# A sign bit carried through a float64-to-float32 conversion: a parametric ReLU on ScalarE in place of an absolute value, and one VectorE operation less

## The chip, the cores and the metric

The kernel runs on one core of one Trainium2 chip. Time is device microseconds (us) of one execution. Before the change the median of three runs is 1049.24 us (1047.91 to 1050.06). In the text PE is TensorE, ACT is ScalarE, DVE is VectorE, POOL is GpSimd, and SP is the engine whose queue issues all DMAs here.

## The reference, cut to what matters

Three stages follow each other: block-causal attention (4 batches, 8 heads, 576 positions, head size 64), a feed-forward layer with h - tanh(h), and a gated layer with an RMS norm in front.

```
scores = where(mask, scale * q @ k^T, -1e9); attn = softmax(scores); x = attn @ v     # q, k, v are float32
h = x @ w_in;  x = (h - tanh(h)) @ w_out                                              # (2304,512)@(512,2048)@(2048,512)
xn = x / sqrt(mean(x*x) + 1e-6) * rms_g
out = (silu(xn @ w_gate) * (xn @ w_val)) @ w_out2                                     # 512 -> 1536 -> 512
```

The weights w_in, w_out, w_gate, w_val and the last w_out arrive as float64. The chip's engines work on float32, so the kernel itself turns each weight into float32 (and then into a rounded high part and a remainder, since nearly every product is computed as three matmuls: high times high, high times low, low times high).

## The kernel before, in words

**The conversion.** A float64 number is read as two 32-bit words. `convert` takes a staged block of 128 x 1024 words, that is 128 x 512 numbers, and runs four operations, each over 128 x 512 elements: ACT multiplies the high word, read as a float, by 2^-112 and takes the absolute value (line 140); ACT scales the low word down to its top three bits (line 142); DVE clamps the first result to a range (line 143), shifts it left by three bits and ors the low bits in (line 144), and then takes the sign bit from the staged high word and ors it in (line 145). The tile `st` is the staging buffer that the DMA of line 129 fills, `cv` holds the intermediate value, `cu` the low bits, and the result lands in `w` (a weight of the first layer), in `fu` (a weight group of the gated layer) or stays in `cv` where the split into high and low part follows in `convert` itself.

**Who calls it.** First-layer weights: 16 blocks of w_in and 16 of w_out, by `convert1`, through the first part of the attention (7 blocks are spread over the first attention unit) and the first pass of the first layer. Gated layer: the 6 pairs of w_out2 blocks during the middle passes, and 12 pairs of w_gate/w_val blocks (one pair is a weight group) around the change from the first layer to the gated one. The class `Convert` loads a pair, converts it, splits it, forms sums of its quarters on POOL (lines 752 to 756), and splits these.

**The stretch that matters late.** The gated layer walks twelve weight groups j. Group 0 to 2 and 10, 11 are used in a form with seven half-size products (`fast`), groups 3 to 9 of the first pass in the plain form with eight (`plain`, 48 matmuls of 384 columns). The weights stand in three slots (`ws`). Groups 3 to 9 are converted while the products run: in step j the kernel fills the slot of group j+2 from the converted pair, writes back what it has split (`keep`, line 774, and `send`, line 782, both DMAs out of `ws` and `wc` to DRAM), converts the second block of group j+3, and loads and converts the first block of group j+4. Groups 10 and 11 are read back from DRAM into their slots (line 1045).

**Order.** PE runs in the order written. ACT, DVE, POOL and SP are placed by a scheduler that simulates a timeline when the program is built; what `pin` wraps keeps its order among pinned instructions. From group 10 of the first pass on, DVE, ACT and POOL run in written order too. All DMAs go through SP, one after the other: a DMA whose data isn't ready holds up those behind it.

Of the kernel before, what the change touches and what calls it, by code (L numbers as in the profile page):

```python
# [10 lines left out]
F32 = mybir.dt.float32  # L11
F32R = mybir.dt.float32r
BF16 = mybir.dt.bfloat16
I32 = mybir.dt.int32
U32 = mybir.dt.uint32
ALU = mybir.AluOpType
AF = mybir.ActivationFunctionType
# [11 lines left out]

REBIAS = 2.0 ** -112  # L30
LOWBITS = 2.0 ** -29 * (1 - 2.0 ** -20)
SIGN = -0x80000000
HIGHEST = float(np.array([0x47EFFFFF], np.uint32).view(np.float32)[0])


# [58 lines left out]
def build(ctx, tc, q, k, v, w_in, w_out, w_gate, w_val, w_out2, rms_g, ident_in, out):  # L94
    nc = tc.nc
    pin = tc.keep_in_program_order
    PE, ACT, DVE, POOL, SP = nc.tensor, nc.scalar, nc.vector, nc.gpsimd, nc.sync
    w_in, w_out, w_gate, w_val, w_out2 = (a.bitcast(I32) for a in (w_in, w_out, w_gate, w_val, w_out2))

    def rnd(eng, o, i):  # L100
        if eng is ACT:
            ACT.activation(out=o, in_=i, func=AF.Copy)  # L102
        else:
            eng.tensor_copy(out=o, in_=i)

    def lo(eng, o, full, hi):
        eng.tensor_tensor(out=o, in0=full, in1=hi.bitcast(F32), op=ALU.subtract)  # L107
# [24 lines left out]
    def convert(st, h, l=None):  # L132

        e = st.rearrange("p (e t) -> p e t", t=2)
        low, high = e[:, :, 0], e[:, :, 1]
        t = wk.tile([128, 512], I32, name="cv", tag="cv")
        u = wk.tile([128, 512], I32, name="cu", tag="x2s")
        f = t.bitcast(F32)

        pin(ACT.activation(out=f, in_=high.bitcast(F32), func=AF.Abs, scale=REBIAS))  # L140

        pin(ACT.activation(out=u, in_=low.bitcast(U32), func=AF.Copy, scale=LOWBITS, bias=-0.5))
        pin(DVE.tensor_scalar(f, f, HIGHEST * REBIAS, 0.0, ALU.min, ALU.max))
        DVE.scalar_tensor_tensor(t, t, 3, u, ALU.logical_shift_left, ALU.bitwise_or)
        DVE.scalar_tensor_tensor(h.bitcast(I32) if l is None else t, high, SIGN, t, ALU.bitwise_and, ALU.bitwise_or)
        if l is None:
            return
        rnd(ACT, h, f)
        lo(DVE, l, f, h)
# [445 lines left out]
    with tc.manual_schedule(engines={PE.engine}):  # L595
# [37 lines left out]
        def convert1(n):  # L633

            j, half = divmod(n, 2)
            if half == 0:
                t = w1tile(0, j)
                convert(staged.pop(n), t[:, 0:512], t[:, 512:1024])
                SP.dma_start(out=w1d[0][j], in_=t.bitcast(F32))
                wi[j] = t  # L640
                return
            if j % 2 == 0:
                wo["new"] = w1tile(1, j + 1, F32)
            t = wo["new"]
            o = t[:, 512 * (j % 2):512 * (j % 2) + 512]
            convert(staged.pop(n), o)
            wo[j] = o
            if j % 2:
                SP.dma_start(out=w1f[j // 2], in_=t)
# [84 lines left out]
        class Convert:  # L734
# [8 lines left out]
            def piece(self, part):  # L743
                if part == 0:
                    self.f = env["cvp"].tile([128, 2, 512], F32, name="fu", tag="fu", bufs=2)
                convert(self.st[part], self.f[:, part])
# [145 lines left out]
        for s in range(NSA):  # L892
# [32 lines left out]
            h = env["t"].tile([128, 512], F32, name="t", tag="t")[:, 0:TG]  # L925
# [385 lines left out]
```

## Time and profile before

| | |
|---|---|
| median of three runs | 1049.24 us |
| profiled execution, its own time | 1049.75 us |
| its span in the profile | 1048.0 us |
| PE busy | 1025.0 us, 98% |
| DVE busy | 782.4 us, 75% |
| ACT busy | 665.3 us, 63% |
| POOL busy | 351.4 us, 34% |

The span is the time from the first to the last instruction that the profile shows; the execution's own time has 1.75 us more around it. Busy shares are means over stages that differ, so the table of stretches and the waits of each engine matter more than the totals. A row of waits says which instruction waited, for which one, for how long in total, how often, and the longest.

### The profile page before, as it was taken

What the parts mean: (1) busy time and instruction counts of PE and PEld (TensorE: products, weight loads), DVE (VectorE), ACT (ScalarE), POOL (GpSimd) and SP (SyncE); (2) the same over time, 40 slices, a digit from 0 to 9 for tenths busy, and PEclk for the clock granted to TensorE, in tenths of its full rate; (3) what the DMA queues carried; (4) which work ended last, traced back from release to release, by engine and by line L of the source; (5) the groups of instructions that cost most, each with busy time, mean ns of one, the idle gap of its engine ahead of it and who ended that gap; (6) DMA issues with size and microseconds to landing.
All of it is one profiled execution on the core that took longest, in us unless ns stands there. A gap on an engine that the chain in (4) does not pass through costs nothing.

```text
span 1048.0 us, 18044 instructions
## 1 busy us (share of the span) xinstructions
PE 1025.0 (98%) x6014; PEld 934.5 (89%) x6014; DVE 782.4 (75%) x1557; ACT 665.3 (63%) x1533; POOL 351.4 (34%) x467
## 2 busy tenths in 40 slices
PE   8899999999999999999999999999999999999998
PEld 5666678998889889998999989998999999999998
DVE  5988857776787786778667989877876678666775
ACT  6977768788888877788858675543742147422253
POOL 5622111123343233424332544347211281111710
PEclk9999999999999999999999999999999999999999
DMA  9898898989787699768859978799697757876664
GB/s 215 272 293 296 263 301 261 277 224 287 203 231 193 152 268 279 210 204 260 295 162 340 372 281 330 262 350 347 241 345 270 273 196 262 299 278 247 257 218 145
DMA packets 190958, 274.03 MB, mean 261 GB/s; under 512 B 109456, under 2 KB 151184, under 8 KB 184464
## 3 DMA queue, kind: packets, MB, share of 16 engines
q1 hardware_dynamic: 190864, 272.87, 79.4%
q8 instruction: 48, 0.79, 0.3%
q14 instruction: 46, 0.38, 0.1%
HBM read 209.39 MB, written 63.44 MB: 260 GB/s over the span
## 4 chain that ended last, share of the span: by engine, by line
PE 74%; DVE 9%; DMA 8%; ACT 5%; issue 3%; POOL 1%; SPq 1%; DVEq 0%; POOLq 0%; ACTq 0%
PE t L930 5%; PE t L482 5%; PE t L932 5%; PE t L931 5%; PE acc L706 4%; PE acc L708 4%; PE acc L707 4%; PE gv L1026 4%; PE gv L1028 4%; PE gv L1027 4%; PE t L526 3%; PE acc L716 3%; PE ga L708 2%; PE ga L706 2%; PE ga L707 2%
## 5 line engine op out<-in xcount | busy, mean ns | idle before, releaser
L930 PE MATMUL t<-xh,w 128*128 128x384 f32 x384 | 137.3, 357 | 1.5 <-DVE pp L107 1.4
L932 PE MATMUL t<-xh,w 128*128 128x384 f32 x384 | 129.6, 338 | 0.0
L931 PE MATMUL t<-xl,w 128*128 128x384 f32 x384 | 129.3, 337 | 0.0
L1026 PE MATMUL gv<-xh,ws 128*128 128x384 f32 x308 | 103.5, 336 | 2.7 <-DMA ws<-w2d 2.4
L1028 PE MATMUL gv<-xh,ws 128*128 128x384 f32 x308 | 103.4, 336 | 0.0
L1027 PE MATMUL gv<-xl,ws 128*128 128x384 f32 x308 | 103.4, 336 | 0.0
L706 PE MATMUL acc<-w,gh 128*128 128x512 f32 x240 | 98.6, 411 | 1.2 <-ACT gh L102 0.9
L497 ACT ACTIVATE pt<-pt,stat 128x64 f32<-128x64 f32 (+2 forms) x144 | 80.3, 559 | 25.9 <-DVE pt L495 24.9
L708 PE MATMUL acc<-w,gl 128*128 128x512 f32 x240 | 95.0, 396 | 0.6 <-DVE gl L107 0.6
L707 PE MATMUL acc<-w,gh 128*128 128x512 f32 x240 | 94.4, 393 | 0.0
L1080 ACT ACTIVATE gt<-c 128x384 f32<-128x384 f32 x29 | 15.2, 524 | 116.7 <-DVE c L1079 116.7
L1083 POOL TENSOR_TENSOR g<-va,vb 128x384 f32<-128x384 f32 x29 | 31.8, 1095 | 150.0 <-ACT va L1082 150.0
L495 DVE TENSOR_SCALAR_CACHE_REDUCE pt<-t 128x64 f32<-128x64 f32 (+2 forms) x144 | 64.0, 449 | 19.7 <-PE t L482 18.8
L930 PEld LDWEIGHTS t<-xh,w 128*128 128x128 f32 x384 | 72.3, 188 | 5.8 <-DVE pp L107 1.8
L931 PEld LDWEIGHTS t<-xl,w 128*128 128x128 f32 x384 | 72.4, 189 | 2.3
L932 PEld LDWEIGHTS t<-xh,w 128*128 128x128 f32 x384 | 72.0, 188 | 0.0
L102 ACT ACTIVATE pp<-t 128x512 fp32r<-128x512 f32 (+6 forms) x152 | 63.0, 436 | 11.7 <-PE t L526 11.3
L526 PE MATMUL t<-ident,pt 128*128 128x128 f32 x400 | 65.7, 274 | 2.2 <-POOL pt L511 2.2
L107 DVE TENSOR_TENSOR gl<-gt,gh 128x384 fp32r<-128x384 f32 x80 | 55.4, 693 | 15.5 <-ACT gh L102 15.1
L107 DVE TENSOR_TENSOR pp<-t,pp 128x512 fp32r<-128x512 f32 (+3 forms) x112 | 55.0, 509 | 14.9 <-ACT pp L102 14.4
L107 POOL TENSOR_TENSOR vp<-vr,vp 128x640 fp32r<-128x640 f32 (+1 forms) x24 | 33.7, 1406 | 95.0 <-ACT vp L102 89.1
L526 PEld LDWEIGHTS t<-ident,pt 128*128 128x128 f32 x400 | 50.5, 140 | 16.4 <-issue 5.1
(210 smaller groups left out, 3183.1 us busy)
## 6 DMA issues: line engine op xcount, KB each, us to landing
ws<-w2d SPq DMA_DIRECT2D x26, 1792.0 KB, 7.3
w<-w1d_i SPq DMA_DIRECT2D x68, 512.0 KB, 5.5
ws<-wod SPq DMA_DIRECT2D x21, 1536.0 KB, 6.4
w<-w1d_o SPq DMA_DIRECT2D x52, 512.0 KB, 5.1
st<-in_moe_w_out SPq DMA_DIRECT2D x28, 512.0 KB, 4.5
w2d<-wc SPq DMA_DIRECT2D x9, 1024.0 KB, 6.6
st<-in_moe_w_in SPq DMA_DIRECT2D x16, 512.0 KB, 5.1
w1d_i<-w SPq DMA_DIRECT2D x16, 512.0 KB, 5.0
```

What stands on the lines that cost most here:

```text
L107: eng.tensor_tensor(out=o, in0=full, in1=hi.bitcast(F32), op=ALU.subtract)
L497: ACT.activation(out=pt[:, 0:keys], in_=pt[:, 0:keys], func=AF.Exp, scale=-1.0, bias=least, accum_out=st[:, 8 + ti:9 + ti])
L526: PE.transpose(t[:, (j - a) * 128:(j - a + 1) * 128], pt[:, j * 128:(j + 1) * 128], ident)
L706: PE.matmul(acc, lhsT=gh[:, c], rhs=wh, start=first, stop=False, skip_group_check=more)
L707: PE.matmul(acc, lhsT=gh[:, c], rhs=wl, start=False, stop=False, skip_group_check=more)
L708: PE.matmul(acc, lhsT=gl[:, c], rhs=wh, start=False, stop=last, skip_group_check=more)
L930: PE.matmul(h, lhsT=wh[:, c], rhs=xh[:, kk], start=(kk == 0), stop=False)
L931: PE.matmul(h, lhsT=wh[:, c], rhs=xl[:, kk], start=False, stop=False)
L932: PE.matmul(h, lhsT=wl[:, c], rhs=xh[:, kk], start=False, stop=(kk == KD - 1))
L1026: PE.matmul(ps, lhsT=wh[:, c], rhs=xh[:, kk], start=(first and kk == 0), stop=False)
L1027: PE.matmul(ps, lhsT=wh[:, c], rhs=xl[:, kk], start=False, stop=False)
L1028: PE.matmul(ps, lhsT=wl[:, c], rhs=xh[:, kk], start=False, stop=(last and kk == nk - 1))
```

## The change: what it does

The absolute value becomes a parametric ReLU with slope 2^32 for negative inputs. A positive high word gives the same value as before. A negative one gives a value that is 2^32 times as large in size, so bit 28 of the result is set, besides its own sign bit. The shift by three moves bit 28 to bit 31, the place of the sign, and drops the old sign bit. The clamp gets a negative lower bound for that reason. The operation of line 145 goes, and line 144 writes its result where line 145 wrote it.

```diff
-SIGN = -0x80000000
+NEGATIVE = 2.0 ** 32
...
-        pin(ACT.activation(out=f, in_=high.bitcast(F32), func=AF.Abs, scale=REBIAS))
+        pin(ACT.activation(out=f, in_=high.bitcast(F32), func=AF.Prelu, scale=REBIAS, alpha=NEGATIVE))
 
         pin(ACT.activation(out=u, in_=low.bitcast(U32), func=AF.Copy, scale=LOWBITS, bias=-0.5))
-        pin(DVE.tensor_scalar(f, f, HIGHEST * REBIAS, 0.0, ALU.min, ALU.max))
-        DVE.scalar_tensor_tensor(t, t, 3, u, ALU.logical_shift_left, ALU.bitwise_or)
-        DVE.scalar_tensor_tensor(h.bitcast(I32) if l is None else t, high, SIGN, t, ALU.bitwise_and, ALU.bitwise_or)
+        pin(DVE.tensor_scalar(f, f, HIGHEST * REBIAS, -HIGHEST * REBIAS * NEGATIVE, ALU.min, ALU.max))
+        DVE.scalar_tensor_tensor(h.bitcast(I32) if l is None else t, t, 3, u, ALU.logical_shift_left, ALU.bitwise_or)
```

Since the sign no longer comes from `st`, the staging buffer's last readers are now the two ACT operations. The scheduler places the rest anew: PE keeps its order entirely, ACT has the same instructions in another order (the five loads of activation tables among them), and POOL and SP are reordered as well. Line numbers behind line 144 are one lower in the changed kernel.

On DVE, the last weight group that is converted beside the products (group 9), before; `fu` is the converted pair, `ws` a slot, and `g_7` the result of group 7:

```order
L143 TENSOR_SCALAR cv<-cv 128x512
L144 SCALAR_TENSOR_TENSOR cv<-cv,cu 128x512
L143 TENSOR_SCALAR cv<-cv 128x512
L145 SCALAR_TENSOR_TENSOR fu<-st,cv 128x512
L1102 TENSOR_TENSOR g_7_8480<-ga,gt 128x384
L144 SCALAR_TENSOR_TENSOR cv<-cv,cu 128x512
L145 SCALAR_TENSOR_TENSOR fu<-st,cv 128x512
L107 TENSOR_TENSOR ws<-fu,ws 128x1024
L1102 TENSOR_TENSOR g_7_8510<-gv,gt 128x384
L107 TENSOR_TENSOR wc<-fu,wc 128x1024
```

The same place now:

```order
L143 TENSOR_SCALAR cv<-cv 128x512
L1101 TENSOR_TENSOR g_6_8340<-gv,gt 128x384
L144 SCALAR_TENSOR_TENSOR fu<-cv,cu 128x512
L143 TENSOR_SCALAR cv<-cv 128x512
L1101 TENSOR_TENSOR g_6_8370<-gv,gt 128x384
L144 SCALAR_TENSOR_TENSOR fu<-cv,cu 128x512
L107 TENSOR_TENSOR ws<-fu,ws 128x1024
L107 TENSOR_TENSOR wc<-fu,wc 128x1024
L1101 TENSOR_TENSOR g_7_8412<-ga,gt 128x384
```

Two operations are gone, and the conversion of group 9 now stands beside the results of group 6 where it stood beside those of group 7.

On SP's queue, the end of the same stretch, before; `w2d_80` and `w2d_81` are the copies in DRAM of groups 8 and 9, `w2d_82` and `w2d_83` those of groups 10 and 11, and `xn` is the next block of activations:

```order
L774 DMA w2d_80<-ws 256x1x768
L1045 DMA ws<-w2d_82 128x3584
L774 DMA w2d_81<-ws 256x1x768
L782 DMA w2d_80<-wc 256x1x1024
L782 DMA w2d_81<-wc 256x1x1024
L1045 DMA ws<-w2d_83 128x3584
L828 DMA xn<-x2d 128x512
L829 DMA xn<-x2d 128x2x256
```

The same place now:

```order
L773 DMA w2d_80<-ws 256x1x768
L781 DMA w2d_80<-wc 256x1x1024
L1044 DMA ws<-w2d_82 128x3584
L773 DMA w2d_81<-ws 256x1x768
L827 DMA xn<-x2d 128x512
L781 DMA w2d_81<-wc 256x1x1024
L828 DMA xn<-x2d 128x2x256
L1044 DMA ws<-w2d_83 128x3584
```

The write of group 8's second part moved ahead of the load of group 10, and two loads of `xn` moved ahead of the load of group 11.

## Rows read from the trace of the kernel before

**Rows 1.** The page, busy time of each engine over the span.

```profile
PE 1025.0 (98%) x6014; PEld 934.5 (89%) x6014; DVE 782.4 (75%) x1557; ACT 665.3 (63%) x1533; POOL 351.4 (34%) x467
```

**Rows 2.** Stretches: window, length, busy us of PE, PEld, DVE, ACT, POOL, clock, DMA.

```profile
17.00:48.00 31.00, 25.72 (x164) 18.61 (x164) 27.73 (x94) 29.20 (x96) 21.73 (x45) 1.00 1.03 272
650.00:700.00 50.00, 49.46 (x283) 49.14 (x282) 41.18 (x52) 26.09 (x41) 21.92 (x22) 1.00 0.79 283
700.00:720.00 20.00, 17.58 (x100) 17.29 (x101) 12.41 (x17) 5.59 (x11) 17.26 (x17) 1.00 1.00 379
```

**Rows 3.** PE's waits, 17 to 50 us: waiter, releaser, us in total, times, longest.

```profile
PE t L579 <- ACT pp L102: 3.5, 4, 1.3
PE t L526 <- POOL pt L511: 2.2, 3, 1.3
```

**Rows 4.** PE's waits, 600 to 730 us.

```profile
PE gv L1026 <- DMA ws<-w2d: 2.4, 1, 2.4
PE acc L706 <- ACT gh L102: 0.9, 1, 0.9
PE acc L708 <- DVE gl L107: 0.6, 2, 0.3
PE ga L1028 <- DVE ws L107: 0.5, 1, 0.5
```

**Rows 5.** PE's waits, 350 to 600 us.

```profile
PE t L930 <- DVE pp L107: 1.4, 1, 1.4
```

**Rows 6.** Line 145: ns min/median/max, first and last start, shape.

```profile
L145 DVE SCALAR_TENSOR_TENSOR fu<-st,cv x36: 644/685/1819, 275.0 to 696.8; 128x512 int32<-128x512 int32 x36
L145 DVE SCALAR_TENSOR_TENSOR cv<-st,cv x16: 662/682/961, 21.3 to 134.5; 128x512 int32<-128x512 int32 x16
L145 DVE SCALAR_TENSOR_TENSOR w<-st,cv x16: 674/685/1098, 26.9 to 141.0; 128x512 int32<-128x512 int32 x16
```

**Rows 7.** DVE by line, 17 to 50 us: count, busy us, mean ns, idle before.

```profile
L145 DVE SCALAR_TENSOR_TENSOR cv<-st,cv 128x512 int32<-128x512 int32 x3 | 2.2, 727 | 0.0
L145 DVE SCALAR_TENSOR_TENSOR w<-st,cv 128x512 int32<-128x512 int32 x3 | 2.0, 683 | 0.0
```

**Rows 8.** Lines 140 and 836 on ACT: ns min/median/max.

```profile
L140 ACT ACTIVATE cv<-st x68: 642/669/743, 16.9 to 694.0; 128x512 f32<-128x512 f32 x68
...
L836 ACT ACTIVATE xn<-xn,rinv x18: 704/711/738, 563.7 to 892.1; 128x512 f32<-128x512 f32 x18
```

**Rows 9.** DVE in order of time, at 384 us: start, us, what.

```profile
384.25 0.68 DVE L145 SCALAR_TENSOR_TENSOR fu<-st,cv 128x512 int32<-128x512 int32 x1
...
385.55 0.65 DVE L107 TENSOR_TENSOR pp<-t,pp 128x512 fp32r<-128x512 f32 x1
```

**Rows 10.** DVE in order of time, groups 8 and 9.

```profile
686.90 0.69 DVE L145 SCALAR_TENSOR_TENSOR fu<-st,cv 128x512 int32<-128x512 int32 x1
...
696.78 0.69 DVE L145 SCALAR_TENSOR_TENSOR fu<-st,cv 128x512 int32<-128x512 int32 x1
...
705.09 1.23 DVE L107 TENSOR_TENSOR wc<-fu,wc 128x1024 fp32r<-128x1024 f32 x1 [2.90 <-ACT wc L761]
```

**Rows 11.** SP's queue in order of time.

```profile
687.65 0.37 SPq L129 DMA_DIRECT2D st<-in_moe_w_val  x1
...
706.96 0.70 SPq L1045 DMA_DIRECT2D ws<-w2d  x1
```

**Rows 12.** ACT in order of time, group 9's second block.

```profile
693.95 0.67 ACT L140 ACTIVATE cv<-st 128x512 f32<-128x512 f32 x1 [1.74 <-DMA st<-in_moe_w_val]
694.52 0.66 ACT L142 ACTIVATE cu<-st 128x512 int32<-128x512 uint32 x1
```

**Rows 13.** PE in order of time, first matmul of group 11.

```profile
717.97 0.42 PE L1026 MATMUL gv<-xh,ws 128*128 128x384 f32 x1 [2.42 <-DMA ws<-w2d]
```

**Rows 14.** SP's waits, 600 to 720 us.

```profile
SPq L129 <- DVE fu L145: 36.6, 12, 5.3
SPq L828 <- DMA w2d<-wc: 4.8, 2, 3.3
```

## The prediction

> **What bounds the kernel now.** I read the busy totals first. PE is busy 1025.0 of 1048.0 us; DVE, where the change takes work away, is busy 75% [rows 1]. So nearly all of what DVE saves is hidden under PE, and the change is worth what it takes from the 23 us in which PE stands still. The second view is therefore the list of PE's waits, by stretch, with the conversions in mind: these run from 17 to 141 us (first-layer weights) and in pieces from 275 to 697 us [rows 6].
>
> In the first attention unit PE loses 3.5 us to ACT and 2.2 to POOL [rows 3]. The table of stretches says who is late there: ACT is busy 29.20 of 31.00 us, DVE 27.73 [rows 2]. Between 350 and 600 us there is one wait of 1.4 us for DVE [rows 5]. Between 600 and 730 us, where the gated layer's weights are converted beside the products, PE waits 2.4 us for a DMA that loads a slot, 0.9 and 0.6 for ACT and DVE at the end of the first layer, and 0.5 for a split by DVE [rows 4]. In between PE is full, and DVE work there is free.
>
> Third, for these places, I read the engines in order of time, backwards from PE's wait to what was late. The longest one (2.4 us) ends when group 11's weights land, at 717.97 us [rows 13]. Their load left SP at 706.96 [rows 11], 11.0 us before, although the slot's last user, group 8, was through some 8 us earlier (worked out below). SP had not come to it: ahead of it in the queue stands the write of group 9's second part, whose data DVE finished only at 705.09 + 1.23 = 706.3 [rows 10]. So this wait is the tail of the conversion of group 9.
>
> **The change part by part.**
>
> *The removed operation.* 36 + 16 + 16 = 68 times a DVE operation of 0.685 us (median) goes [rows 6], 46.6 us of DVE. Directly on PE's path it stands only where a wait above ends behind it.
>
> *First unit, 17 to 48 us.* Six of them run here, 2.2 + 2.0 = 4.2 us [rows 7]. ACT's work is not reduced, and it fills all but 31.00 - 29.20 = 1.8 us [rows 2]. That is the upper bound of the gain. The lower bound is a loss of about 1: ACT's order is new here, and in it ACT takes the rounding of a converted weight a little sooner, where it can stand waiting for DVE. I take 1.0, nearer to the upper bound, since DVE at 27.73 of 31.00 us is so full that most of what ACT waits for will run through it.
>
> *First pass to 150 us, and 250 to 600 us.* The wait of 1.4 us at 384 us ends behind a run of DVE work: line 145 at 384.25, one more operation, then the awaited split at 385.55 [rows 9]. The 0.68 us of line 145 come out of that path; with the overlap of neighbours I take 0.6, between 0 (the new order puts something else there) and 1.4 [rows 5]. Everywhere else in these stretches PE's order is the same and ACT's and DVE's is partly new, so a wait of the size of the others in the lists, 1 to 2 us, can come or go; I count 0, and ±2 for the range.
>
> *End of the first layer, 600 to 650 us.* 0.9 + 0.6 us of waits for splits of the first layer [rows 4], with conversions among them on DVE. I take 0.7 of these 1.5, between 0 and 1.5. A loss of 1 is possible: behind the square root of the norm ACT now has two conversions, where it had one, before the next product's evacuation, and each can wait for its DMA (1.74 us in the row shown) [rows 12].
>
> *Groups 3 to 9.* Here the removed operation did one thing more: it was the last reader of the staging buffer. The load of the next block was issued at 687.65, right behind line 145 at 686.90 + 0.69 = 687.59 [rows 10, 11]; SP waited for that operation 12 times, 36.6 us in all [rows 14]. The loop of one group is: load issued 687.65, ACT starts on it at 693.95 [rows 12], DVE's line 145 at 696.78 [rows 10], next load. From 686.90 to 696.78 that is 9.88 us per group. PE needs 48 matmuls per group, 48 x 50 / 283 = 8.5 us [rows 2]. So the conversion falls back 1.4 us per group against PE, until PE waits for it (the 0.5 us) and the write behind it holds up SP (the 2.4 us). Without line 145 the buffer is free when ACT is through, at 694.52 + 0.66 = 695.2: the loop would be 695.2 - 687.65 = 7.5 us, shorter than PE's 8.5. PE then sets the pace, and the conversion stays ahead.
>
> How far ahead? Over the last four groups alone 4 x 1.4 = 5.6 us, so group 9's second part would be written at about 701 where it was 706.4, and the load of group 11 would leave by 701.5. Group 8's products end at about 699: 717.97 less the wait of 2.42 is 715.5, and two groups before it (9 with 48, 10 with 42 matmuls) take 90 x 0.177 = 15.9 us, with 0.5 of waiting. So the slot is free by then. With the same 11.0 us to land it is there at 712.5, and PE wants it at 715.0. What speaks against the whole 2.4: the DMA engines are full from 700 to 720 us (share 1.00) [rows 2], and the new SP order puts two loads of activations ahead of the load of group 11. I take 2.0 of the 2.4 (bounds 0 and 2.4), and 0.5 of the 0.5.
>
> *The new function on ACT.* The trace has no Prelu. Nearest rows of the same shape: the absolute value it replaces, 669 ns, and a scaling with the factor read from a tile, 711 ns [rows 8]. So a Prelu costs between 0 and 42 ns more; I take 0, since its slope is given as a number, as the scale is. The upper end, 7 x 42 ns = 0.3 us in the ACT-bound first unit, goes into the range. The Trainium skill (ScalarE: Activation LUTs, section What ACT_TABLE_LOAD costs) says that a function costs the same per element whatever it is, and that each operand read through a pointer adds about 93 ns. The two rows agree in direction and show less than half of that, 42 ns. By the page, an alpha that went in as a pointer would add 7 x 93 ns = 0.65 us in the first unit, an estimate from that page, and the sum below would be 1045.2 instead.
>
> *Sum.* 1.0 + 0.6 + 0.7 + 0.5 + 2.0 = 4.8 us. The profiled execution took 1049.75 us, its span and 1.75 us around it; less 4.8 that is 1044.95. The median of the runs is 0.5 below the profiled one, so I put the forecast between, at 1044.7.
>
> **The rivals.**
>
> *Hidden anyway.* PE is 98% busy, ACT bounds the start whatever DVE does, and the DMA engines at share 1.00 deliver group 11 no sooner, because what is issued earlier only joins a full queue. Then remain 0.6 + 0.5 and part of the first unit, 1.5 us in all: 1048.0. For it speaks the DMA row of 700 to 720 us; against it, that the share is 0.79 from 650 to 700 us [rows 2], so there is room to move the bytes forward.
>
> *All of it, and more.* If every term comes out at its upper end, and the new order takes 1.5 of the ±2 as well, the sum is 1.8 + 1.4 + 1.5 + 0.5 + 2.4 + 1.5 = 9.1 us: 1040.6. Several independent places would all have to come out well.
>
> *Slower: SP's queue.* The load of group 11 now stands behind a load of `xn`, which reuses a buffer that the write of group 8's second part must have left. SP waited for such writes before, 4.8 us over 2 times, 3.3 the longest [rows 14], but behind the load of group 11. If that wait now comes ahead of it and the conversion has not become earlier, the load leaves 3.3 us later than 706.96, and PE's wait grows from 2.4 to 5.7; the later slots, whose loads queue behind it on full DMA engines, can add as much again. With nothing gained elsewhere that is 1053 to 1056. It decides from the point at which the load of group 11 leaves SP later than 707 us.
>
> *The change doesn't do what it says*: if Prelu belonged to another set of ACT's tables, every conversion between exponentials would reload tables. The order has five such loads before and after, so I give it no chance of its own.
>
> **How the numbers follow.** Forecast (the conversion stays ahead, 1041.5 to 1047.1) 0.55; hidden anyway (1047 to 1050) 0.25; more (below 1041.5) 0.09; slower by the queue (above 1051) 0.11. What a measurement of this kernel can tell from no change is about 0.2%, 2.1 us: faster means below 1047.1, slower above 1051.3. Faster: 0.53 of the forecast, the 0.09, and 0.05 from the edge of the hidden case, 0.67. Same: the remaining 0.22. Slower: 0.11. For eight in ten the range goes from 1040.5 to 1050: it leaves out the slower case and some of the best one.
>
> **What would show it.** Right: PE's wait for the slot of group 11 is under 0.5 us, the load of that slot leaves before 703 us, and SP's wait for the conversion before a staging load is down from 36.6 us to well under 20, now on ACT. In the first unit ACT is busy over 95% of a stretch about 1 us shorter. DVE's busy total is down by 45 to 50 us, ACT's within 3 us of 665. Wrong: a Prelu over 720 ns; waits of PE at new places between 250 and 600 us that add to over 3 us; or the same 2.4 us for the slot though its load left earlier, which would make the DMA engines the cause.

## The result, and the profile after

The changed kernel takes 1040.28 us (median of 4 runs, 1039.26 to 1042.98); the kernel before, beside it, 1049.04 (1047.91 to 1050.06). The ratio is 0.9909, 95% interval 0.9891 to 0.9928: 8.8 us faster, where 4.5 were forecast. The direction was right and the size half of what came; the time lies just below the range.

The page of the changed kernel, busy time of each engine:

```profile
PE 1023.0 (98%) x6014; PEld 934.2 (90%) x6014; DVE 736.3 (71%) x1489; ACT 666.3 (64%) x1533; POOL 342.9 (33%) x467
```

Against [rows 1], DVE has 68 instructions and 46.1 us less, ACT 1.0 us more, PE the same 6014. The new function is no dearer than the old one. Its line on ACT (count, then ns min/median/max) against [rows 8]:

```profile
L140 ACT ACTIVATE cv<-st x68: 643/663/697, 14.7 to 675.3; 128x512 f32<-128x512 f32 x68
```

PE's waits from 600 to 730 us, which [rows 4] listed with 2.4 us for a DMA at their head:

```profile
PE ga L705 <- DVE va L1080: 1.0, 1, 1.0
PE acc L707 <- DVE gl L107: 0.3, 1, 0.3
PE acc L705 <- ACT gh L102: 0.2, 1, 0.2
```

The DMA wait is gone, and so are most of the waits at the end of the first layer; a wait of 1.0 us for the gate's arithmetic is new. From 350 to 600 us, where [rows 5] had one wait, the list is empty now.

SP's queue shows why the slot is in time (start, duration, what); the first row is the load of the last staged block, the second the load of group 11:

```profile
668.45 0.37 SPq L129 DMA_DIRECT2D st<-in_moe_w_val  x1
...
693.81 0.33 SPq L1044 DMA_DIRECT2D ws<-w2d  x1
```

In [rows 11] these left at 687.65 and 706.96. SP's waits from 600 to 720 us, against the 36.6 us of [rows 14]:

```profile
SPq L129 <- ACT cu L142: 16.9, 9, 3.9
...
SPq L1044 <- PE gv L1027: 8.4, 2, 5.4
...
SPq L827 <- DMA w2d<-wc: 5.8, 1, 5.8
```

The staging load now waits for ACT, and half as long. The write that the slower rival feared is waited for 5.8 us, but this wait ends at 686 us, where it holds up nobody. The load of group 11 now waits for PE's last matmul on its slot (the row of line 1044): PE sets the pace.

The stretches of [rows 2] in the changed kernel (window, length, busy us of PE, PEld, DVE, ACT, POOL, granted clock, DMA share, GB/s):

```profile
17.00:48.00 31.00, 26.21 (x148) 18.05 (x147) 23.93 (x83) 26.34 (x87) 17.27 (x40) 0.89 1.03 280
650.00:700.00 50.00, 50.00 (x287) 50.00 (x286) 30.64 (x37) 21.86 (x35) 30.29 (x29) 1.00 0.91 332
700.00:720.00 20.00, 18.99 (x114) 18.75 (x113) 13.77 (x19) 5.02 (x11) 8.95 (x8) 1.00 0.72 276
```

From 650 to 700 us PE is full, and DVE's 41.18 us are down to 30.64: the conversion is ahead. The DMA engines carry more from 650 to 700 us and are no longer full behind it. The first row is the one that went the other way: PE waits there at least as much as before, and for part of it the clock was at the lower level (1.2 GHz). PE's waits from 17 to 50 us, against [rows 3]:

```profile
PE t L578 <- ACT pp L102: 4.1, 4, 1.7
PE t L525 <- DVE xl L107: 1.3, 1, 1.3
...
PE t L525 <- POOL pt L510: 0.3, 1, 0.3
```

The waits for POOL went from 2.2 to 0.3 us, but 1.3 of this only changed its name: the last transpose of the unit waits as long as before, now with a split on DVE (`xl`) as the last thing that ends. Before, then now:

```profile
48.53 0.30 PE L526 MATMUL t<-ident,pt 128*128 128x128 f32 x1 [1.27 <-POOL pt L511]
```

```profile
49.83 0.30 PE L525 MATMUL t<-ident,pt 128*128 128x128 f32 x1 [1.27 <-DVE xl L107]
```

The waits for ACT grew from 3.5 to 4.1. Most of that is the first one. ACT takes the rounding of a converted weight (`w`) earlier now, ahead of the second rounding of `pp`, for which PE waits; before, it came behind. Before, then now:

```profile
20.49 0.85 ACT L102 ACTIVATE pp<-t 128x384 f32<-128x384 f32 x2
...
22.38 0.62 ACT L102 ACTIVATE w<-cv 128x512 fp32r<-128x512 f32 x1
```

```profile
18.67 0.62 ACT L102 ACTIVATE w<-cv 128x512 fp32r<-128x512 f32 x1
19.19 0.48 ACT L102 ACTIVATE pp<-t 128x384 f32<-128x384 f32 x1
```

PE's wait there grew from 0.95 to 1.47 us, and behind it the granted clock fell in this profile: it is 0.83 from 17 to 27 us. From 27 to 37 us, with the next long wait, it is 0.83 again. Ten us at 0.83 are 1.7 us lost, so 3.4 us went in this profile.

### The profile page after: what moved, and what is told of

It is laid out like the page before. It is cut to its first block, busy times and chain, and to the rows that moved or that the text cites. A ratio compares the mean times of both kernels' runs of the same rounds, so it can differ in the third digit from the quotient of the medians.

```text
span 1041.1 us, 17914 instructions
## 1 busy us (share of the span) xinstructions
PE 1023.0 (98%) x6014; PEld 934.2 (90%) x6014; DVE 736.3 (71%) x1489; ACT 666.3 (64%) x1533; POOL 342.9 (33%) x467
## 4 chain that ended last, share of the span: by engine, by line
PE 86%; DVE 5%; ACT 4%; DMA 2%; issue 1%; POOL 1%; SPq 1%; DVEq 0%; ACTq 0%; POOLq 0%
PE t L929 6%; PE t L931 6%; PE t L930 5%; PE t L481 5%; PE gv L1026 5%; PE gv L1027 5%; PE gv L1025 5%; PE acc L705 4%; PE acc L707 4%; PE acc L706 4%; PE acc L715 4%; PE t L525 4%; PE ga L1025 3%; PE ga L1027 3%; PE ga L1026 3%; PE ga L707 2%
## 5 line engine op out<-in xcount | busy, mean ns | idle before, releaser
L496 ACT ACTIVATE pt<-pt,stat 128x64 f32<-128x64 f32 (+2 forms) x144 | 80.5, 560 | 26.8 <-DVE pt L494 26.3
L494 DVE TENSOR_SCALAR_CACHE_REDUCE pt<-t 128x64 f32<-128x64 f32 (+2 forms) x144 | 64.2, 451 | 28.2 <-PE t L481 26.8
L102 ACT ACTIVATE pp<-t 128x512 fp32r<-128x512 f32 (+6 forms) x152 | 63.4, 436 | 11.5 <-PE t L525 10.8
```

The source lines that it names most:

```text
L496: ACT.activation(out=pt[:, 0:keys], in_=pt[:, 0:keys], func=AF.Exp, scale=-1.0, bias=least, accum_out=st[:, 8 + ti:9 + ti])
```

## The experiments

Both kernels were profiled again first, since two single profiles also differ by what varies from run to run.

**The changed kernel again** (no edit).

> The changed kernel once more. Its first profile gained 1.4 us in the first attention unit less than nothing: PE was ahead by 2.7 us at 14 us and behind by 1.9 at 33 us, in two stretches of 3.4 us (from 19.8 and from 30.0 us) in which the granted clock was at half. Theory: these drops are a matter of the single run, and the first unit is worth about 1 us without them; then this profile has one such stretch at most, a clock of 0.997 or more, PE between 0 and 2 us ahead of the kernel before at 48 us, and the time is about 1040. Rival: the drops belong to the changed order of the first unit; then they stand at the same places again and PE is 1 to 2 us behind at 48 us.

Measured: 1039.79 us (1039.40 to 1040.55, 6 runs), before 1051.26 (1047.75 to 1056.32, 23 runs), ratio 0.989 (0.9871 to 0.9908). This profile is the theory's case: the clock is full from 17 to 48 us, and at 48 us PE is 2.0 us ahead of the first profile of before and 0.4 ahead of the third, which follows. The rival is not gone, though. Over all profiles here, seven are of kernels that drop the operation from every block of the first layer; in them the wait of 1.47 us at 19 us is 1.2 to 2.2 us long, and in five the clock from 17 to 27 us is 0.83 or less. In the nine others that wait is 0.95 us, and the clock is 1.00 there. So the early part of the change costs clock in some executions; that the longer wait is the reason is likely, and no run shows it apart.

**The kernel before again, twice** (no edit).

> The kernel before, profiled again. Theory: part of the gain is clock. The waits of before at 384 us (1.4), about 618 us (1.5 in two pieces) and 715 us (2.4) put TensorE's granted clock to the half level for 3.4 or 6.8 us behind them in some of its executions, each for 1.7 or 3.4 us of loss; then this profile shows at least one such stretch behind one of these waits, and its end lies 1.7 to 5 us later than in the first profile for that reason. Rival: the clock stays at full level behind these waits, as in the first profile, and the whole gain is work and waiting; then every start on PE agrees with the first profile within 1 us from 50 us on, but for the stretch before 14 us.

> The kernel before, profiled once more, as the run before this one: theory, at least one stretch at the half level behind a wait of 1.4 us or more after 48 us in one of the two; rival, none in both.

Measured: 1051.44 and 1048.83 us. Both cases of the theory are there, one in each profile. The stretch behind the wait for group 11, first in the dearer one, then in the other:

```profile
716.00:724.00 8.00, 5.82 (x25) 5.86 (x26) 6.46 (x7) 1.38 (x4) 7.06 (x7) 0.79 1.04 418
```

```profile
716.00:724.00 8.00, 7.35 (x42) 7.38 (x43) 7.79 (x9) 1.13 (x4) 6.76 (x6) 1.00 1.05 424
```

Here PE had waited 2.6 us for the slot in the first and 1.5 in the second; behind the longer wait the clock was partly at the lower level. So the waits of the kernel before cost clock in some executions. Of the 74 runs of this kernel that stand beside the experiments, 20 had the full granted clock over the whole run (median 1049.5), 54 did not (median 1051.3). The 1.8 us between the groups hold the longer waits as well as the clock behind them. Whether the change gains clock on the whole is not shown: its own ten executions had a granted clock of 0.996 to 0.999, with the same median as the 74 (0.998). Against the 20 with the full clock the median of the ten, 1040.0, is 9.5 us faster.

For the rest I compare the third profile of before with the second of the changed kernel: no half level between 14 and 1036 us in either, 1048.83 against 1039.55 us. PE executes its instructions in the same order in all kernels here, so the start of one and the same matmul can be compared. The table gives by how much each stretch (in the time of the kernel before) became shorter (-) or longer (+) against the third profile of before:

```
us             forecast  changed  late   1 column  256 columns  op kept,
                          kernel   only   by DVE     by DVE     no hold
14 to 48          -1.0     -0.2    +0.2     -1.1       -0.7      -0.6
48 to 250          0       -1.6    -1.6     -1.7       -1.3      -2.2
250 to 310         0       -1.0    -1.0     -0.9       -0.2      +1.5
310 to 400        -0.6     -1.8    -1.9     -1.9       -1.4       0.0
400 to 600         0       -0.3    -0.3     -0.4       -0.3      +3.6
600 to 645        -0.7     -2.3    -2.4     +1.6       -0.5      -2.5
645 to 700        -0.5     -0.7    -0.7     -0.7       -0.8      -0.7
700 to 760        -2.0     -1.1    -1.0     -1.0       -1.0      -0.3
```

The second column of figures adds to -9.0; the forecast adds to -4.8. The other columns are the experiments below. Three of their entries hold about 1.7 us of lower clock each: one column from 600 to 645 us, and the operation kept from 250 to 310 and from 400 to 600 (a clock of 0.83 over 10 us in each). Of the stretch from 48 to 250 us, 1.3 us are not the change's: the first profile of before, of the same program, is that much shorter there than the third, which has a wait of 1.1 us at 142 us that the first lacks.

**Only the gated layer's 36 conversions changed, and only the first layer's 32.** One branch in the helper and a flag in its callers:

```
+    def convert(st, h, l=None, old=False):
+        if old: (lines 140 to 145 of before)  else: (the new ones)
...
-            convert(staged.pop(n), o)
+            convert(staged.pop(n), o, old=True)     # late only
...
-                convert(self.st[part], self.f[:, part])
+                convert(self.st[part], self.f[:, part], old=True)     # early only
```

> Only the 36 conversions of the gated layer are changed; the 32 of the first layer keep the absolute value and the operation that ors the sign in. Theory (the gain lies in the late stretches, 250 to 725 us, where PE's shift in the two traces grows from -0.4 to -7.5 us): 1041 to 1043. Rival (the first 150 us carry half of the gain, hidden in the profiled run by the clock): 1044 to 1046.

> Only the 32 conversions of the first layer are changed. Theory (late stretches): 1047 to 1049, at most 2 us faster than before. Rival (the first 150 us carry half of it): 1043 to 1046. If the two parts add, this gain and that of the late part make up about 9 us.

Measured: late only 1040.95 us, ratio 0.9901 (0.9882 to 0.9921); early only 1048.31, ratio 0.9975 (0.996 to 0.999). Nearly all of the gain is the gated layer's. (The two gains, 10.3 and 3.0 us, add to more than the 11.5 of the changed kernel beside them.) With the early ones alone the slot wait of before stands where it stood (PE in order of time: start, duration, what, idle before), and in that profile the clock fell behind it:

```profile
717.18 0.66 PE L1034 MATMUL gv<-xh,ws 128*128 128x384 f32 x1 [3.14 <-DMA ws<-w2d]
```

```profile
716.00:724.00 8.00, 6.82 (x24) 6.86 (x25) 5.05 (x6) 0.49 (x1) 5.60 (x5) 0.57 1.04 425
```

**The sign or-ed in twice** (the kernel before, with one more of the removed operation):

```
+        DVE.scalar_tensor_tensor(t, high, SIGN, t, ALU.bitwise_and, ALU.bitwise_or)
```

> The kernel before with the sign or-ed in twice: 68 operations of 0.69 us more on DVE, and the staging buffer held 0.7 us longer. If the gain of the change is a slope (every such operation on the chain of conversion costs what it cost), 8 to 14 us slower than before, 1057 to 1063, with PE's waits at groups 7 to 11 grown. If the change removed something that stood there once (a threshold), under 4 us slower.

Measured: 1077.17 us, ratio 1.0268 (1.0253 to 1.0284). That is 26.8 us more than the 1050.34 of the runs of before beside it: one operation more costs two and a half to three times what one less gives. About 10 us of it are clock: in its profile the granted clock is 0.76 from 168 to 182 us and from 746 to 760, and 0.83 from 394 to 404 and from 698 to 708; twice 14 x 0.24 and twice 10 x 0.17 make 10.1 us. **One operation less still** (the changed kernel without its clamp):

```
-        pin(DVE.tensor_scalar(f, f, HIGHEST * REBIAS, -HIGHEST * REBIAS * NEGATIVE, ALU.min, ALU.max))
```

> The changed kernel without the clamp (line 143), so without the limits on very large numbers: 68 DVE operations of 0.43 us fewer again. If DVE is still on PE's path somewhere, 2 to 5 us faster than the changed kernel; by its trace the gated stretch has no PE wait left that ends with DVE, so I expect 0 to 2 us, 1038 to 1041.

Measured: 1039.72 us, ratio 0.9912 (0.9897 to 0.9926), no faster than the changed kernel, though DVE is busy 22 us less (714.2). So the curve is steep on one side and flat on the other: where the conversions keep ahead of PE, less DVE time gave nothing more.

**What the earlier release is worth.** The first trial added a one-column copy of the staging buffer, to be its last reader:

```
+        DVE.tensor_copy(out=hold, in_=high[:, 0:1])
```

> The changed kernel, with a one-column copy out of the staging buffer on DVE behind the shift, so that the buffer is held till DVE is through, as before, while the removed operation stays removed (68 small copies are added instead). Theory A (the operation's own time on DVE is what counts): 1040 to 1042, PE's wait for the slot of group 11 gone as well. Theory B (the early release of the staging buffer is what lets the conversions keep ahead between 640 and 720 us): the period of a group is between 8.5 and 9.9 us, some of the waits at groups 9 and 11 come back, 1042 to 1045.

Measured: 1050.7 us, ratio 0.9986 (0.9969 to 1.0002). It tells nothing on the release: nothing tied the copy to the end of the conversion, so it was scheduled in front of it, and DVE stood there for the loads (idle time of DVE before the copy, by releaser, us and times):

```profile
  DMA st<-in_moe_w_out: 20.3, 18
```

The second trial keeps the whole DVE time but lets the buffer go: line 145 reads another tile.

```
-        DVE.scalar_tensor_tensor(h..., high, SIGN, t, ALU.bitwise_and, ALU.bitwise_or)
+        DVE.scalar_tensor_tensor(h..., u, 0, t, ALU.bitwise_and, ALU.bitwise_or)
```

> The changed kernel with an idle operation of the same kind and size on DVE in place of the removed one (the low bits and-ed with zero, or-ed into the result), which does not read the staging buffer. So DVE has its old work and the buffer is still released early. Theory A (DVE's time counts): 1046 to 1050. Theory B (the release counts): 1041 to 1044.

Measured: 1047.17 us, ratio 0.9967 (0.9951 to 0.9983): theory A's range. The last trial takes the time and keeps the hold, by or-ing the sign in once more on a few columns behind the shift, which depends on its result:

```
+        DVE.scalar_tensor_tensor(o[:, 0:1], high[:, 0:1], SIGN, o[:, 0:1], ALU.bitwise_and, ALU.bitwise_or)
```

> The changed kernel with the sign or-ed in once more, on one column of 512, behind the shift: a DVE operation of about 0.15 us that reads the staging buffer last, so that the buffer waits for DVE as before, while nearly all of line 145's time is gone. Theory A (half of the late gain is the earlier release of the buffer): the gated layer's weights are again later; from 310 us to the end this kernel gains 3 to 4 us on the kernel before, where the changed kernel gains 6 to 7; 1043 to 1046 us. Theory B (only the DVE time counts): it gains as the changed kernel does, 0.15 x 36 = 5 us of DVE aside; 1039.5 to 1041.5 us, and SP still waits for DVE in front of the staging loads.

> The same with the sign or-ed in again on 256 columns of 512: release by DVE, about 0.39 us of the 0.69 kept. Theory A: as the last reader on DVE costs about half of the gain and the kept time half of the rest, 1046 to 1048 us. Theory B: half of the DVE time is gone and so about half of the gain comes, 1044 to 1046 us. Rival to both (a threshold: the conversion either keeps ahead of PE or not): within 1 us of the changed kernel or of the kernel before, nothing between.

Measured: 1 column 1044.89 us, ratio 0.9957 (0.9944 to 0.997); 256 columns 1046.06, ratio 0.9963 (0.9949 to 0.9977). The times lie in theory A's ranges (for 256 columns at the edge of A's and of B's), B's for one column did not come, and nothing jumped. From 310 us to the end the one-column kernel gains 2.4 us (1.0 + 0.7 + 0.4 + 1.9 - 1.6 in the table), where the changed one gains 6.2; about 1.7 of the difference is clock. But the table says more than either theory: the release and the time pay at different places.

The wait at 384 us goes by the time, in these profiles. In order: operation kept with the buffer free, 256 columns, one column.

```profile
PE t L930 <- DVE pp L107: 1.4, 1, 1.4
```

```profile
PE t L932 <- DVE pp L108: 0.7, 1, 0.7
```

```profile
PE t L932 <- DVE pp L108: 0.2, 1, 0.2
```

The end of the first layer, 600 to 645 us, goes by the release: it is gained in full with the operation kept (-2.5), hardly with 256 columns (-0.5), and not with one (+1.6, about as much as the clock cost there: 0.83 from 614 to 624 us). There the held buffer delays the blocks, and SP waits for DVE nearly as long as before, though the operation takes 0.15 us:

```profile
SPq L130 <- DVE fu L147: 32.7, 13, 5.0
```

ACT then stands in line for the late block (ACT in order of time, one-column kernel):

```profile
614.23 1.06 ACT L763 ACTIVATE ws<-fu 128x1024 fp32r<-128x1024 f32 x1 [2.24 <-POOL fu L758]
615.20 0.47 ACT L940 ACTIVATE gt<-t 128x384 f32<-128x384 f32 x1
...
617.05 0.52 ACT L103 ACTIVATE gh<-gt 128x384 fp32r<-128x384 f32 x1 [0.26 <-DVE gt L946]
```

The rounding of the converted block (line 763) waits 2.24 us for POOL's part of it, and `gt` and `gh` of the first layer are queued behind it. PE waits for that `gh`:

```profile
617.63 0.50 PE L708 MATMUL acc<-w,gh 128*128 128x512 f32 x1 [2.69 <-ACT gh L103]
```

The slot of group 11, at last, goes by the time as well. With one column its load left SP at 696.78 us and landed 14.0 us later, and PE waited 0.04 us for it; with 256 columns PE did not wait. With the operation kept and the buffer free PE waits as long as in the third profile of before:

```profile
701.32 0.66 SPq L1045 DMA_DIRECT2D ws<-w2d  x1
```

```profile
715.68 0.42 PE L1026 MATMUL gv<-xh,ws 128*128 128x384 f32 x1 [1.69 <-DVE g L1085]
```

The list names `g`, which ended at the same time (715.60); but the matmul reads `xh` and `ws`, and the load of `ws` landed 14.2 us after its issue, at 715.5. In the third profile of before it left at 706.52 and landed 10.0 us later: an issue 5.2 us earlier brought the landing forward by 1.0, with the DMA engines full at either time (share 1.02 from 700 to 720 us in both). The reason stands in the pace of the conversions. Each weight group is staged in two blocks. The loads of the first block of the last four groups left SP at these times (us); the last figure is their mean distance:

```
before (first profile)            657.72  666.09  677.00  685.86   9.4
changed (first profile)           640.59  647.36  657.84  665.45   8.3
1 column by DVE                   651.08  659.19  667.43  675.92   8.3
operation kept, buffer free       647.20  655.93  663.71  675.64   9.5
```

With the time gone the conversions go at 8.3 us a group, held buffer or not; with the time kept, freeing the buffer did not quicken them.

**SP's queue by itself** (the kernel before, the write of group 9's second part issued by POOL):

```
-                    pin(SP.dma_start(out=w2d[self.j][:, :, n], in_=w.bitcast(F32)))
+                    eng = POOL if self.j == 9 else SP
+                    pin(eng.dma_start(out=w2d[self.j][:, :, n], in_=w.bitcast(F32)))
```

> The kernel before with one DMA moved from SP's queue to POOL's: the write of the second part of group 9's converted weights, which SP waited for in front of the load of group 11. No work is taken away. Theory (SP stood still for the late conversion): the load of group 11 leaves SP before 703 us (706.96 before), PE's wait of 2.4 us for its slot falls under 0.5, and the kernel is 1.5 to 3 us faster than before, ratio 0.997 to 0.9985. Rival (the DMA engines are full and set the landing): the load leaves early, lands as late as before, PE waits 2 us or more, ratio 0.999 to 1.001.

Measured: 1053.15 us (1048.95 to 1057.05), ratio 1.0016 (0.9999 to 1.0033). The load of group 11 left at 703.53 instead of 706.96, as the theory had it, and PE's wait for the slot fell to 0.2 us. But the load took 13.3 us to land, at 716.8, where before it landed at 717.9 (first profile) and 716.5 (third): the wait was short because PE came 1.2 to 1.6 us later. In this the rival was right: the load left early and landed about as late as before. The gain did not come. SP, then POOL, in order of time:

```profile
703.53 1.14 SPq L1046 DMA_DIRECT2D ws<-w2d  x1
```

```profile
707.78 0.82 POOL L783 DMA_DIRECT2D w2d<-wc  x1 [2.66 <-DVE wc L107]
```

SP did not wait for the late data any more, but for its write: the next load of `xn` takes over a buffer that this write must have left, and from POOL it went out at 707.78 and took 11.2 us to land. SP's waits from 709 to 722 us:

```profile
SPq L829 <- DMA w2d<-wc: 13.3, 2, 7.1
```

The load of `xn` left at 719.08, and behind it stands the load of the output product's first slot:

```profile
720.13 1.01 SPq L1049 DMA_DIRECT2D ws<-wod  x2
```

It left 5.6 us later than in the first profile of before (714.50), landed 8.1 us after, and PE waited for it:

```profile
728.32 0.55 PE L706 MATMUL ga<-ws,gh 128*128 128x256 f32 x1 [3.82 <-ACT va L102]
```

The list names ACT, whose `va` ended at the same time; but the matmul reads `ws` and `gh`, and 720.13 + 8.1 = 728.2 is the load. The clock was at 0.66 from 724 to 734 us. This is the mechanism of my slower rival, the load of `xn` that waits for a write of converted weights, and it decides where that write is late: a queue in which a late transfer waits has only been changed for another. In the changed kernel the conversion, and with it the write, is early.

**Two edits of the changed kernel**, meant to gain more: `EARLY = 5` in place of 7 (fewer conversions in the first unit), and a third more of the first unit's roundings on DVE in place of ACT:

```
-                    rnd(ACT if u.group or ti % 3 else DVE, hv[:, a:z].bitcast(F32), tv)
+                    rnd(ACT if u.group or ti % 3 == 2 else DVE, hv[:, a:z].bitcast(F32), tv)
```

> The changed kernel with 5 conversions in the first attention unit in place of 7; the other two move into the first pass of the first layer. Theory (ACT bounds the first unit, busy 94% there): two conversions are 2 x (0.66 + 0.66) us of ACT and a rounding of 0.6, so 1.5 to 3 us less in the first unit, part of it given back where ACT is 75% busy: 1037 to 1040. Rival (the unit is bound by the chain from PE to DVE to ACT to POOL and back, not by ACT's sum): no change, 1040 to 1042.

> The changed kernel with one more third of the first unit's probability roundings moved from ACT to DVE, which has room there since the change (26.2 of 31.0 us busy in the second profile of the changed kernel, ACT 27.8). Theory (the first unit still waits for ACT: 4.1 us of PE waits for ACT pp): PE's waits for pp fall by 1 to 2 us and the kernel takes 1038 to 1039.5 us, ratio to before 0.988 to 0.9905. Rival (the chain of one head's steps sets the unit, not ACT's total): the waits move to DVE and the time stays at 1039.8, ratio 0.989 to 0.9915.

Measured: 1039.6 us, ratio 0.9904 (0.9891 to 0.9917), and 1044.07 us (1040.32 to 1046.52), ratio 0.9922 (0.9897 to 0.9947). Neither beats the changed kernel, and the second is about 4 us slower by its median, with a granted clock of 0.993 to 1.000. With the roundings moved, PE's waits from 14 to 50 us only changed their names:

```profile
PE t L578 <- ACT pp L102: 2.1, 2, 1.9
PE t L525 <- POOL pt L510: 1.5, 2, 1.3
PE t L578 <- ACT pt L496: 1.4, 1, 1.4
```

## Why the prediction was half right

*The removed operation, 46.6 us of DVE, almost all hidden.* Right: 46.1 us went.

*The new function at no cost.* Right: 663 ns against 669. The Trainium skill (ScalarE: Activation LUTs, section What ACT_TABLE_LOAD costs) says that a function costs the same per element whatever it is; these two lines agree. The 42 ns that I took for a factor read from a tile came from two lines that differ in more, since line 140 reads every second word of its block. Line 856 (855 in the changed kernel), SBUF to SBUF in the same shape with an immediate factor, takes 617 ns in the kernel before (median of 27), and line 836 takes 711: the factor costs 94 ns. The 1045.2 for that case should have been 1044.7 + 0.65 = 1045.4.

*First unit, 1.0 us.* Wrong: 0.2 in the clean pair, less than two profiles of the same kernel differ by there (0.8 between the first and the third of before). The step took ACT's spare 1.8 us as the bound and thought DVE's relief would pass through ACT. What the relief did was to make the converted weight ready sooner, so that ACT rounded it ahead of the `pp` for which PE waits: 0.5 us more of waiting at 19 us, while waits further on became shorter. My lower bound had this earlier rounding, but with ACT waiting for DVE in it; it is the rounding's own 0.62 us that PE waits for. The clock behind that wait, 1.7 us each time, was in no term. Moving work from ACT to DVE did not help, so ACT's total was not the bound either.

*"Everywhere else ... I count 0", and 0.6 of the 1.4 us at 384 us.* This is one of the steps that failed. From 250 to 600 us the change gave 3.1 us. PE's waits there, third profile of before, then second of the changed kernel:

```profile
PE t L930 <- DVE pp L107: 1.4, 1, 1.4
PE t L482 <- DVE pp L107: 1.4, 1, 1.4
PE t L559 <- DVE pp L107: 0.5, 1, 0.5
PE t L482 <- DVE pt L495: 0.4, 1, 0.4
```

```profile
PE t L481 <- DVE pp L107: 1.4, 1, 1.4
...
PE t L929 <- DVE pp L107: 0.2, 1, 0.2
PE t L481 <- DVE pt L494: 0.2, 1, 0.2
```

All are waits for DVE. The one at 384 us fell by 1.2, nearly twice the duration of the line 145 in front of it, and 0.7 went in a stretch from 250 to 350 us whose waits I had not listed. With 256 columns half of it was left. One removed operation in front of a wait is not the measure here: 1.2 us is more than one of them lasts. That the second is the line 145 ten microseconds earlier is likely; no run shows it apart.

*End of the first layer, 0.7 of 1.5.* Another step that failed: 2.3 us came. I argued from DVE's time and took half of it for safety. The trials show another cause: it is the release of the buffer, which I had put to work for groups 3 to 9 only. The waits were there to be read (0.9 for ACT, 0.6 for DVE, and 0.3 at 645 us for `xlu`, which [rows 4] leave out); all but 0.5 us of them went. The remaining 0.9 us of the 2.3 stand in no list.

*Groups 3 to 9: 0.5 and 2.0.* What I forecast for the queue came: SP's wait moved to ACT and halved, the load of group 11 left before 703 us, no DMA wait is left, and PE sets the pace. The step that explains it failed: I let the release of the buffer shorten the loop to 7.5 us. In the trials the release alone leaves it at 9.5 us and PE waiting 1.7 us for the slot; the time alone, with SP still waiting 32.7 us for DVE, brings it to 8.3. The lead was off as well: I had worked out 5.5 us from the last four groups, and between the first profiles the load of group 11 came 13.2 us sooner (706.96 to 693.81). By the loads of the first blocks the conversions were 17.1 us ahead at the first of these groups and 20.4 at the last, so most of the lead was there before them. The same 11.0 us to land was no constant either: 10.0 to 14.2 us in these profiles. The sum is smaller than mine: in the clean pair 0.7 and 1.1, since there only 1.5 of DMA wait was there to gain, and 1.0 came back as the new wait for `va`. The page showed neither: the slot wait of before varies from profile to profile (2.4, 2.6, 1.5).

*Hidden anyway* falls with the empty wait lists. Its reason is real, though: with the operation kept, and in the queue experiment, the load of group 11 left 5.2 and 3.0 us before that of the third profile of before, and landed 1.0 us earlier and 0.3 later. In the second profile of the changed kernel it left at 691.23, landed 10.7 us later and was there 4.9 us before PE came to it. *Slower by SP's queue* did not come either: the write was waited for 5.8 us, but early. Its mechanism is real, as the queue experiment shows with 7.1 us; it needs the late write that the change does away with. *All of it, and more*, which I gave 0.09 and put at 1040.6, is what came, though not by its terms: the first unit gave next to nothing, groups 3 to 9 gave less than their upper ends, and the end of the first layer and 310 to 400 us gave more than theirs. That the total lay so near is luck.

*The median.* The sum was made against a profile with the full clock from 17 us to the end (its first 14 us were 2.1 to 2.4 us longer than in the two later ones of the same kernel), and the forecast left the clock out. In other executions of the same program the waits of before are followed by the lower level, and in the changed kernel the first unit's are.

What stays open: how the 250 to 310 us (1.0) divide among the operations removed there, and the 1.6 us from 48 to 250, of which most varies from run to run. Open, too, is the part of the order: the scheduler placed each of these kernels anew, so that time, hold and order changed together, and no run keeps the order of before with the operation gone. What goes by the time and what by the release is read from one profile of each trial.

## What to carry to other kernels

When an operation goes from an engine whose lateness PE waits for, list every wait of PE for that engine, small ones too, and do not take the half of each: here one of them fell by nearly twice what the operation in front of it lasts. An operation that is the last reader of a loaded buffer has two prices, its time and its hold, and they are paid at different places; try both by themselves before saying which it was. And the side matters: here one operation more cost 27 us (some 10 of it clock), one less gave 9 to 11, and one less again gave nothing, so measure where on that curve a kernel stands before a removal is priced.

## What the runs showed of the hardware

TensorE's granted clock fell to the lower level (1.2 GHz) behind some of PE's longer waits and not behind others of the same size. Around a wait of 3.1 us it stood at 0.57 from 716 to 724 us, around one of 2.6 at 0.79, around one of 2.4 and one of 1.5 at 1.00; but the changed kernel's first profile has 0.89 from 17 to 48 us with waits of up to 1.7 us, and its second, with the same waits, 1.00:

```profile
17.00:48.00 31.00, 24.87 (x156) 17.98 (x156) 26.24 (x88) 27.83 (x90) 18.91 (x43) 1.00 1.09 293
```

So kernels with such waits spread from execution to execution: the kernel before from 1047.39 to 1056.32 us (74 executions), the changed one from 1039.26 to 1042.98 (ten), the one with the moved roundings from 1040.32 to 1046.52 (six).

Where the DMA engines were full or nearly so (share 0.89 to 1.02 from 700 to 720 us), an earlier issue moved the landing little: in three profiles the load of group 11's slot took 10.0 us to land when it was issued at 706.52, 13.3 when issued at 703.53, and 14.2 when issued at 701.32.
